# Prologue of a delta-rule and feed-forward kernel: order of its first loads, stores and solves changed, the second solve one step earlier

## The chip, the cores and the metric

The kernel runs on one core of one Trainium2 chip. The metric is the device time of one execution in microseconds (us); the time of a kernel is the median of several executions. A core has TensorE for matrix products (PE in the rows, its weight loads apart as PEld), VectorE (DVE), ScalarE (ACT), GpSimd (POOL) and SyncE (SP). Each engine runs its own instructions in order, and each of SP, ACT and POOL can also issue DMA transfers; an engine that waits, for a semaphore or for room to issue a transfer, holds up all that stands behind on it.

## The reference

```python
# attention, for every batch b and head h (B=4, H=8, S=768, D=48)
k_n = k / (norm(k) + 1e-6)
for t in range(S):
    y[:, :, t] = q[:, :, t] @ state
    v_old = state^T k_n[:, :, t]
    state = state + beta[t] * outer(k_n[:, :, t], v[:, :, t] - v_old)
x = y as (B*S, H*D) = (3072, 384)
# first feed-forward
h = maximum(x @ w_in, 0); x = (h * h) @ w_out          # 384 -> 2048 -> 384
# second feed-forward
h = maximum(maximum(x @ w1, x @ w2), x @ w3)           # 384 -> 768
out = h @ w_out2                                       # 768 -> 384
```

All of it is float32.

## The kernel before

**Tiling.** The 768 positions are cut into 12 chunks of 64, and the recurrence within a chunk becomes triangular algebra: products K K^T and Q K^T of the chunk (`kk_matmul`, L160), a solve of the strict triangle in blocks of 32 (`solve`, L243/L245, 30 pairs of small VectorE operations, scaled at L246), and a few small products with the running state `Sb`. The chunks are solved two at a time (`HALVED`): pair 0 is chunks 0 and 1, pair 1 is chunks 2 and 3, and so on. A chunk is 256 rows of the feed-forward, 64 positions of 4 batches. The heads of a chunk are worked in two halves, p=0 and p=1.

**From K K^T to a solve.** A `kc` load (L149) brings one half of a chunk's keys and queries; `kk_matmul` forms the products; ACT copies K K^T out of PSUM (L175) and VectorE masks Q K^T (L176); K K^T is stored in device memory (`kk`, L164) and so is Q K^T (`p`, L181). `start32` reads `kk` back in the layout of the solve, `buf<-kk` (L262, the "M loads", four for a pair), and `prep` takes the diagonal (`ss`, L224), forms norms (L195 to L208), selects the strict triangle on GpSimd (L213) and scales (L214). After the solve, `finish32` stores the result as `xt` (L278), and each chunk's attention loads it as `xb` (L294).

**Attention of a chunk.** `load_x` and `load_att` load `k` (L291), `xb` (L294), `kq` (L306), `v` (L308), `p` (L310) and `ktp` (L312). Then come the products with the 32-blocks (`pZ` L344, transpose L340, copy L346; `pW` L354, copy L356), `st0` (scaled v L361; for chunks from 1 on `pA`, `pY` from the state L372, and r = v - pA L375), `mm_u` (pU L382, u L383), `st2` (pY L395, pD L400, state update L404/L406, yy L410) and `st3` (transpose L416, and the split of the result into `xh`, `xl`, L419/L420). In `attention` the two halves are worked one after the other, p=0 to its yy before p=1 starts at its `mm_u`.

**First feed-forward.** `moe_a(c)` works the 256 rows of chunk c: for eight pieces fp of 256 hidden columns, `s1` forms the products with `win` (L446), ACT takes relu, square and the high part (`gg`, `p`, `gh`, L451 to L453), VectorE the low part (`gl`, L454), and `s2` multiplies with `wout` (L465). A float32 matrix product is made of three products of high and low parts, so each weight is first split: `convert` (L81 to L100) takes five VectorE operations (L93, L96, L97, L98, L100) and two on ACT (L90, L99) for a piece of 128 columns. The result is stored as `x` (L477), twice per step; twelve steps, one for each chunk, follow each other. The second feed-forward (L619 to L677) starts behind them.

**What sets the order.** In the prologue: K K^T of pair 0, the first `NE` = 5 conversions of `win`, solve of pair 0, attention of chunk 0, the other `win` conversions. Then `steps(moe_a(c), ...)` interleaves step c with generators at given rates: attention of chunk c+1, `wout` conversions in step 0, K K^T of a pair (`KK`), the solve of a pair (`SOLVE`), and from step 9 on the conversions of `w3` weights (`w3load`). A scheduler with a timeline then orders the instructions of each engine by what it thinks is ready; `behind(a, b)` adds an order between two instructions without data. The transfers issued by SP and by ACT share eight semaphores in turn, so an issue also waits for the transfer eight issues before it to have landed; those of POOL have eight of their own.

Pair 0 is done in the prologue. In the kernel before, pair 1 has its K K^T in step 0 and its solve in step 1 (rate 8). Chunk 2's attention, which needs that solve, stands in step 1 too, begun late and at rate 1.3, and its end is in step 2. The scheduler may take conversions of `w3` earlier than their step, where it finds room:

Of the kernel before, what the change touches and what calls it, by code (L numbers as in the profile page):

```python
# [17 lines left out]
NC = S // C  # L18
# [17 lines left out]
def delta_moe(ctx, tc, kc, ab, kt, vt, beta, beta32, beta16, kq, w_in, w_out, w1, w2, w3, w_out2, out):  # L36
# [32 lines left out]
    NR, NRP = 3, 9  # L69
# [11 lines left out]
    def convert(src, hi, lo, shape, lo_eng, dma):  # L81
# [18 lines left out]
        lo_eng.tensor_tensor(out=lo, in0=l.bitcast(F32), in1=hi.bitcast(F32), op=ALU.subtract)  # L100
# [38 lines left out]
    kcs, nk, p_stored, kk_ends = {}, [0, 0], [], [None, None]  # L139
# [5 lines left out]
    def kkp_load(c, p):  # L145
        k = kcts[nk[0] % len(kcts)]
        nk[0] += 1
        kcs[c, p] = k
        nc.sync.dma_start(k, two(kc, c, p).rearrange("p b q t s -> p (b q) t s"))  # L149
# [13 lines left out]
    def kk_store(c, p, kk, dma):  # L163
        return [dma.dma_start(kk_d[c][:, t, U2 * p:U2 * p + U2], kk[64 * t:64 * t + 64]).ins for t in range(2)]  # L164

    def kkps(cs, ps_, dma=nc.sync):
# [4 lines left out]
        for n, (c, p) in enumerate(todo):  # L171
# [4 lines left out]
            kk_ends[1] = vec.tensor_mul(out=ks[:, 1], in0=pq, in1=mask[:, 1].unsqueeze(1).broadcast_to([128, U2, C])).ins  # L176
            yield
            stores = kk_store(c, p, ks[:, 0], dma)
            for t in range(2):
                o = 64 * t  # L180
                stores.append(nc.sync.dma_start(p_d[c][o:o + 64, U2 * p:U2 * p + U2], ks[64 - o:128 - o, 1]).ins)  # L181
            p_stored[:] = stores[2:]
# [34 lines left out]
    selected = [None]  # L217
# [34 lines left out]
    def start32(g, dma=nc.sync):  # L252
# [21 lines left out]
    def finish32(g, M, dma=nc.sync):  # L274
# [44 lines left out]
    ops, normed = [], []  # L319

    def attention(c):
# [36 lines left out]
        def st0(p):  # L358
# [3 lines left out]
            if c < 2:  # L362
                behind(i.ins, ops[-1])
# [23 lines left out]
        def st2(p):  # L387
            pt_, kt_, u_, pY = (tiles[c, p][i] for i in (3, 4, 7, 8))
            if not c:
                pY = ps_y.tile([128, U2, D], F32, name="pY", tag="y")  # L390
# [16 lines left out]
            yy[p] = att.tile([128, Q, 2, D], F32, name="yy", tag="yy", bufs=1)  # L407
# [18 lines left out]
        for fs in ((st0, 0),), ((zz, k21),), ((ww, 0),), ((mm_u, 0),), ((st2, 0),), ((st0, 1), (st3, 0)), ((mm_u, 1),), ((st2, 1),), ((st3, 1),):  # L426
            for f, p in fs:
                f(p)
                if f is mm_u and p and c + 1 < NC:
# [4 lines left out]
    def moe_a(c, gp):  # L434
# [4 lines left out]
        def s1(fp):  # L439
# [14 lines left out]
            vec.tensor_sub(out=gl, in0=p1, in1=gh.bitcast(F32))  # L454
# [73 lines left out]
    if True:  # L528
# [48 lines left out]
        raw_after[:] = raw_done  # L577
        drain(solve32(0, pool))
        x_after.append(selected[0])
        drain(attention(0))  # L580
        x_after.clear()
# [147 lines left out]
```

## Time and profile before

| | us |
|---|---|
| median of 3 executions | 1062.96 |
| lowest, highest | 1060.36, 1063.26 |
| the profiled execution | 1065.6 |
| span of its profile | 1063.9 |
| PE busy in the span | 933.4 (88%) |
| VectorE busy | 477.6 (45%) |
| ACT busy | 395.1 (37%) |

The span is the time from the first to the last instruction that the profiler saw, 1.7 us less than the execution's own time. The steps of the first feed-forward are marked by their first `x` store. These stores begin at 168.1, 213.6, 291.9, 348.8, 397.8, 455.3, 503.3, 560.2, 620.8, 669.5, 716.9 and 758.7 us, so a step is the time between two of them.

### The profile page before, as it was taken

The numbers are of one execution on the slowest core, as the hardware profiler recorded it, in microseconds if no ns is written. First come the engines' busy times: TensorE is split into PE (matmuls) and PEld (weight loads), VectorE is DVE, ScalarE is ACT, GpSimd is POOL, SyncE is SP. The second block draws the span as 40 slices with busy tenths as digits, with TensorE's granted clock in tenths as the row PEclk, the third lists the DMA queues.
The fourth block names the chain that finished last, engine by engine and source line by source line (L and its number), as shares of the span: only waits on it lengthen the run. The fifth ranks groups of instructions, "written<-read, shape, count | busy, mean of one in ns | idle before, by whom it ended". The sixth has DMA issues, their size and how long they took to land.

```text
span 1063.9 us, 26753 instructions
## 1 busy us (share of the span) xinstructions
PE 933.4 (88%) x11706; PEld 856.9 (81%) x11706; DVE 477.6 (45%) x1057; ACT 395.1 (37%) x780; POOL 125.6 (12%) x200
## 2 busy tenths in 40 slices
PE   4004999959998999899988989998999999999998
PEld 4004898948997999799988979998888888888887
DVE  2799937547223841384257641227352323232221
ACT  2126653423443444344454444455431212121111
POOL 1323010130202020202020202000110000000000
PEclk8555898978999899999998989998999999999999
DMA  9954562552245134514452341104220100000001
GB/s 265 291 122 119 174 177 75 139 139 49 73 128 158 49 95 118 159 53 105 116 165 85 82 144 59 34 9 127 89 75 15 45 16 30 15 16 23 8 23 38
DMA packets 89333, 98.44 MB, mean 93 GB/s; under 512 B 49120, under 2 KB 66784, under 8 KB 89216
## 3 DMA queue, kind: packets, MB, share of 16 engines
q1 hardware_dynamic: 74624, 59.36, 20.3%
q0 software_dynamic: 10496, 31.60, 10.1%
q10 hardware_dynamic: 4096, 5.77, 1.6%
q8 instruction: 92, 1.51, 0.6%
q14 instruction: 25, 0.20, 0.1%
HBM read 71.53 MB, written 25.17 MB: 91 GB/s over the span
## 4 chain that ended last, share of the span: by engine, by line
PE 73%; DVE 10%; DMA 10%; issue 3%; ACT 3%; SPq 1%; POOL 1%; DVEq 0%; ACTq 0%; POOLq 0%
PE p L637 21%; PE p L446 17%; PE px L465 17%; PE po L654 7%; DMA buf<-kk 2%; PE pU L382 2%; DMA kk<-big 2%; DVE buf L243 2%; DVE buf L245 2%; DMA raw<-in_moe_w_dram 2%; PE pk L160 1%; PE pW L354 1%; PE pY L395 1%; PE pZ L344 1%; PE pA L372 1%
## 5 line engine op out<-in xcount | busy, mean ns | idle before, releaser
L465 PE MATMUL px<-gh,wout 128*128 128x256 f32 x1152 | 227.3, 296 | 22.3 <-ACT gh L453 22.3
L465 PEld LDWEIGHTS px<-gh,wout 128*128 128x128 f32 x1152 | 187.0, 200 | 26.2 <-ACT gh L453 23.6
L637 PE MATMUL p<-x_h,w 128*128 128x512 f32 x648 | 203.4, 395 | 0.0
L465 PE MATMUL px<-gl,wout 128*128 128x256 f32 x576 | 170.3, 296 | 5.9 <-DVE gl L454 5.8
L446 PE MATMUL p<-xh,win_h 128*128 128x256 f32 x576 | 169.9, 296 | 0.2
L446 PE MATMUL p<-xl,win_h 128*128 128x256 f32 x576 | 167.3, 294 | 0.0
L446 PE MATMUL p<-xh,win_l 128*128 128x256 f32 x576 | 166.3, 289 | 0.0
L454 DVE TENSOR_TENSOR gl<-p,gh 128x512 fp32r<-128x512 f32 x96 | 65.9, 687 | 175.9 <-ACT gh L453 175.4
L637 PEld LDWEIGHTS p<-x_h,w 128*128 128x128 f32 x648 | 121.6, 188 | 27.1
L637 PE MATMUL p<-x_l,w 128*128 128x512 f32 x324 | 128.1, 395 | 0.0
L451 ACT ACTIVATE gg<-p 128x512 f32<-128x512 f32 x96 | 57.1, 596 | 190.8 <-PE p L446 188.4
L465 PEld LDWEIGHTS px<-gl,wout 128*128 128x128 f32 x576 | 115.3, 200 | 8.4 <-DVE gl L454 7.9
L446 PEld LDWEIGHTS p<-xh,win_h 128*128 128x128 f32 x576 | 114.8, 199 | 1.9 <-ACT xh L419 0.7
L446 PEld LDWEIGHTS p<-xh,win_l 128*128 128x128 f32 x576 | 114.6, 199 | 0.0
L446 PEld LDWEIGHTS p<-xl,win_h 128*128 128x128 f32 x576 | 113.2, 198 | 1.6
L643 DVE TENSOR_TENSOR mx<-p,mx 128x512 f32<-128x512 f32 x36 | 24.9, 691 | 137.1 <-PE p L637 137.1
L637 PEld LDWEIGHTS p<-x_l,w 128*128 128x128 f32 x324 | 61.0, 188 | 14.6
L645 ACT CAST hh<-mx 128x512 fp32r<-128x512 f32 x36 | 22.3, 620 | 130.8 <-DVE mx L644 130.8
L245 DVE TENSOR_TENSOR buf<-buf 128x30 f32<-128x30 f32 (+9 forms) x180 | 59.5, 330 | 5.2
L243 DVE TENSOR_TENSOR buf<-buf 128x30 f32<-128x30 f32 (+9 forms) x180 | 59.2, 329 | 5.4
L452 ACT ACTIVATE p<-gg 128x512 f32<-128x512 f32 x96 | 57.6, 601 | 2.7
L453 ACT CAST gh<-p 128x512 fp32r<-128x512 f32 x96 | 56.1, 585 | 2.7
(132 smaller groups left out, 1362.0 us busy)
## 6 DMA issues: line engine op xcount, KB each, us to landing
kq<-in_kc_dram POOLq DMA_DIRECT2D x22, 448.0 KB, 4.1
raw<-in_moe_w_dram SPq DMA_DIRECT2D x18, 384.0 KB, 4.4
p<-p POOLq DMA_DIRECT2D x24, 256.0 KB, 3.3
raw<-in_moe_w_out_dram SPq DMA_DIRECT2D x13, 384.0 KB, 3.7
buf<-in_kc_dram SPq DMA_DIRECT2D x11, 448.0 KB, 3.8
big<-in_kc_dram SPq DMA_DIRECT2D x11, 448.0 KB, 4.3
v<-in_vt_dram POOLq DMA_DIRECT2D x24, 192.0 KB, 3.9
ktp<-in_kt_dram POOLq DMA_DIRECT2D x24, 192.0 KB, 3.4
```

The lines of the kernel that those rows point to most:

```text
L243: eng.tensor_tensor(out=tv, in0=M[:, 0:j, j].unsqueeze(2).broadcast_to([u, j, m]), in1=M[:, j, j + 1:n].unsqueeze(1).broadcast_to([u, j, m ...
L245: yield eng.tensor_tensor(out=M[:, 0:j, j + 1:n], in0=M[:, 0:j, j + 1:n], in1=tv, op=ALU.add)
L446: pe.matmul(p1[:, j], w[:, k, f], x[c][:, k], start=n == 0 and j == 0, stop=n == 8, skip_group_check=True)
L451: act.activation(out=gg, in_=p1, func=AF.Relu)
L452: act.activation(out=p1, in_=gg, func=AF.Square)
L453: act.copy(gh, p1)
L454: vec.tensor_sub(out=gl, in0=p1, in1=gh.bitcast(F32))
L465: pe.matmul(acc[m], w, x[:, j], start=f == 0 and i == 0 and m != 1, stop=f == NF - 1 and i == 2, skip_group_check=True)
L637: pe.matmul(p, w[i][:, k, fs], x[:, k], start=n == 0, stop=n == 8)
L643: vec.tensor_max(out=t, in0=ps[1], in1=t)
L645: act.copy(hh[:, f], t2)
L654: pe.matmul(po[:, 0:DM], x[:, f, js], w[:, f], start=i == 0, stop=i == 17)
```

## The change

In words, in the order of the program:

- Prologue: `NE` is 4 and not 5. The `kk` stores are all on SP (they were on ACT). The `p` stores of pair 0 move from SP to POOL, behind the triangle's selection. Of the four M loads of solve 0, those of chunk 0 stay on POOL, those of chunk 1 go to SP; the `xt` stores of chunk 0 go to ACT, those of chunk 1 stay on POOL. The first operation of `prep` stands behind the last early conversion, and the later `win` loads behind the last M load.
- The K K^T of pair 1 moves from step 0 into the prologue: its `kc` loads stand behind the last `win` load, its mask operations behind the end of solve 0, and it uses four buffers instead of two.
- The attention of chunk 0 works p=0 and p=1 side by side; the second `pY` and `yy` get places of their own.
- Solve 1 moves from step 1 (rate 8) into step 0 (rate 5, begun after 45 turns, its operations behind the eighth `wout` conversion). The K K^T of the later pairs stay in their steps (`KK` loses its entry for step 0), and chunk 2's attention, in step 1, gets the rate of all others.
- The VectorE part of the `w3` conversions stands behind the last `gl` of step 8; this is lifted for step 11.

```diff
-    def kkps(cs, ps_, dma=nc.sync):
+    def kk_store(c, p, kk):
+        for t in range(2):
+            nc.sync.dma_start(kk_d[c][:, t, U2 * p:U2 * p + U2], kk[64 * t:64 * t + 64])
+
+    def kkps(cs, ps_, late_p=None):
...
+            for i in mul_after:
+                behind(kk_ends[1], i)
...
-        vec.tensor_copy(ss, diagonal(M, n))
+        i = vec.tensor_copy(ss, diagonal(M, n))
+        for j in prep_after:
+            behind(i.ins, j)
...
-                dma.dma_start(M[o:o + 32], units(kk_d[c][..., 32 * s:32 * s + 32], 32 * s, 32))
+                loaded[0] = dmas[i].dma_start(M[o:o + 32], units(kk_d[c][..., 32 * s:32 * s + 32], 32 * s, 32)).ins
...
-                dma.dma_start(units(xt_d[c][..., h], 32 * s, 32), M[o:o + 32])
+                dmas[i].dma_start(units(xt_d[c][..., h], 32 * s, 32), M[o:o + 32])
...
+            order = ((st0, 0), (st0, 1)), ((zz, k21),), ((ww, 0),), ((mm_u, 0), (mm_u, 1)), ((st2, 0), (st2, 1)), ((st3, 0), (st3, 1))
...
-        drain(kkps(HALVED[0], (p1, at), act))
-        NE = 5
+        drain(kkps(HALVED[0], (p1, at), ps_stores))
+        NE = 4
...
+        first_solve = solve32(0, (pool, nc.sync), (act, pool))
...
+        mul_after.append(solved[0])
+        kc_after.append(raws[-1])
+        drain(kkps(HALVED[1], (p1, at)))
...
-        KK, SOLVE = {0: 1, 1: 2, 3: 3, 5: 4, 7: 5}, {1: 1, 2: 2, 4: 3, 6: 4, 8: 5}
+        KK, SOLVE = {1: 2, 3: 3, 5: 4, 7: 5}, {0: 1, 2: 2, 4: 3, 6: 4, 8: 5}
...
-                extra.append((1.3, later(11, attention(c + 1))) if c == 1 else (9 / 15.0, attention(c + 1)))
+                extra.append((9 / 15.0, attention(c + 1)))
...
-                extra.append((8.0 if c == 1 else 5.0, solve32(SOLVE[c])))
+                extra.append((5.0, later(45, solve32(SOLVE[c])) if c == 0 else solve32(SOLVE[c])))
...
             if c == 9:
+                after[:] = last_gl
                 load_w3s = w3load((0, 1))
```

What stands where, at three places. The numbers in the names of tiles tell instances apart: `xt_117` and `kk_93` are chunk 0's, `xt_118` and `kk_94` chunk 1's, `kk_95` and `kk_96` those of chunks 2 and 3; `ksr`, `buf` and `big` are buffers. A line number of the changed kernel is some 4 to 20 higher than that of the same code before.

First place: the stores of solve 0's result for chunk 0 (`xt_117`). On POOL, in the kernel before:

```order
L312 DMA ktp_148<-in_kt_dram 128x384
L306 DMA kq<-in_kc_dram 112x1024 x2
L278 DMA xt_117<-buf 32x32x32 x2
L278 DMA xt_118<-buf 32x32x32 x2
L308 DMA v<-in_vt_dram 128x384 x2
L294 DMA xb<-xt_117 32x16x32 x4
```

On ACT, in the changed kernel, from the norms of solve 0 to the same stores:

```order
L205 ACTIVATE s_401<-ss 128x32
L283 COPY normT<-pt 32x32 x4
L91 ACTIVATE cvt<-big 128x384 x2
L180 COPY buf<-pk 128x512
L180 COPY big<-pk 128x512
L180 COPY ksr_194<-pk 128x512
L291 DMA xt_117<-buf 32x32x32 x2
L180 COPY ksr_195<-pk 128x512
```

The two stores of `xt_117` stood on POOL behind the loads of chunk 0's attention; they stand on ACT now, behind three of the four copies of pair 1's K K^T.

Second place: VectorE in the middle of step 0, where `gl` is written for the feed-forward. Before:

```order
L100 TENSOR_TENSOR wout_1214<-raw,wout_1214 128x384
L97 SCALAR_TENSOR_TENSOR raw<-raw,cvt 128x384
L100 TENSOR_TENSOR wout_1214<-big,wout_1214 128x384
L98 SCALAR_TENSOR_TENSOR raw<-raw 128x384
L454 TENSOR_TENSOR gl<-p_1119,gh 128x512
L93 TENSOR_SCALAR cvt<-cvt 128x384
L96 TENSOR_SCALAR cvt<-cvt 128x384
```

The changed kernel, between its third and fourth `gl` of that step:

```order
L474 TENSOR_TENSOR gl<-p_1246,gh 128x512
L258 TENSOR_TENSOR buf<-buf 128x6x25
L99 SCALAR_TENSOR_TENSOR raw<-raw 128x384
L98 SCALAR_TENSOR_TENSOR raw<-raw,cvt 128x384
L94 TENSOR_SCALAR cvt<-cvt 128x384
L256 TENSOR_TENSOR buf<-buf 128x168
L99 SCALAR_TENSOR_TENSOR raw<-raw 128x384
L97 TENSOR_SCALAR cvt<-cvt 128x384
L258 TENSOR_TENSOR buf<-buf 128x7x24
L101 TENSOR_TENSOR wout_1336<-raw,wout_1336 128x384
L98 SCALAR_TENSOR_TENSOR big<-big,cvt 128x384
```

Solve 1's rows (L256/L258, `buf<-buf`) have come in between the conversions and the `gl`; there are 60 of them, the first ahead of the first `gl`, the last right behind the seventh of eight.

Third place: VectorE where the second half of chunk 2's `r` is written, which PE's pU (L382) waits for. Before, at the turn from step 1 to step 2:

```order
L340 STREAM_TRANSPOSE xT<-xb 128x512
L454 TENSOR_TENSOR gl<-p_2558,gh 128x512
L176 TENSOR_TENSOR big<-pq,mask 128x512
L224 COPY ss<-buf 128x32
L404 TENSOR_TENSOR Sb<-pD,Sb 128x384
L195 TENSOR_SCALAR s_2781<-s_2781 128x32
L196 RECIPROCAL r<-s_2781 128x32
L197 TENSOR_TENSOR r<-r,ss 128x32
L198 TENSOR_TENSOR r<-r,s_2781 128x32
L199 TENSOR_SCALAR nm<-r 128x32
L205 RECIPROCAL r<-nm 128x32
L375 TENSOR_TENSOR r<-v,pA 128x384
```

The changed kernel, in step 1, up to the same `ss`:

```order
L474 TENSOR_TENSOR gl<-p_2310,gh 128x512
L417 TENSOR_TENSOR Sb<-pD,Sb 128x384
L181 TENSOR_TENSOR buf<-pq,mask 128x512
L474 TENSOR_TENSOR gl<-p_2429,gh 128x512
L388 TENSOR_TENSOR r<-v,pA 128x384
L436 TENSOR_TENSOR xl<-pT,xh 128x3x128
L374 TENSOR_TENSOR v<-v,normT 128x384
L474 TENSOR_TENSOR gl<-p_2521,gh 128x512
L181 TENSOR_TENSOR big<-pq,mask 128x512
L353 STREAM_TRANSPOSE xT<-xb 128x512
L474 TENSOR_TENSOR gl<-p_2627,gh 128x512
L235 COPY ss<-buf 128x32
```

Before, this `r` stood behind `ss` and six more operations of solve 2's preparation, and `ss` waits for solve 2's M loads; in the changed kernel the same `r` (its line is 388) stands seven rows ahead of that `ss` (L235), among the `gl` of step 1.

## Rows read from the trace of the kernel before

**Rows 1.** Busy time by engine, PE clock, DMA share and GB/s, in stretches of us.

```profile
core 0: us, PE busy (x) PEld busy (x) DVE busy (x) ACT busy (x) POOL busy (x), PEclk, DMA share, GB/s
24.00:60.00 36.00, 0.37 (x1) 0.10 (x1) 28.84 (x78) 5.93 (x15) 9.56 (x15) 0.50 0.99 268
213.60:266.00 52.40, 37.97 (x688) 35.27 (x682) 31.96 (x87) 16.41 (x37) 10.90 (x17) 0.77 0.37 95
26.60:78.50 51.90, 0.39 (x2) 0.15 (x3) 44.23 (x118) 9.32 (x22) 15.49 (x23) 0.50 0.82 212
78.50:112.00 33.50, 18.36 (x382) 15.98 (x383) 32.47 (x83) 21.76 (x47) 8.28 (x10) 0.50 0.43 130
112.00:168.10 56.10, 52.55 (x998) 50.20 (x998) 32.30 (x74) 31.72 (x67) 7.29 (x11) 0.96 0.55 156
168.10:291.90 123.80, 108.82 (x1718) 103.14 (x1720) 68.31 (x174) 45.11 (x91) 20.61 (x33) 0.88 0.37 97
291.90:397.80 105.90, 100.43 (x1752) 95.56 (x1747) 47.41 (x111) 45.84 (x94) 18.07 (x29) 0.97 0.38 107
...
503.30:560.20 56.90, 52.35 (x1005) 49.63 (x999) 21.35 (x44) 27.39 (x55) 9.65 (x15) 0.97 0.49 139
560.20:620.80 60.60, 54.64 (x781) 50.94 (x774) 42.15 (x113) 28.65 (x61) 8.43 (x14) 0.92 0.35 99
620.80:669.50 48.70, 46.09 (x729) 43.88 (x731) 13.68 (x26) 21.94 (x44) 8.43 (x14) 0.96 0.29 88
```

**Rows 2.** What PE waited for, 0 to 112 us: total, times, longest.

```profile
PE pZ L344 <- DMA xb<-xt: 38.1, 1, 38.1
PE pt L235 <- DVE nm L199: 20.8, 1, 20.8
```

**Rows 3.** Chain of waits, 0 to 112 us: start, duration, what.

```profile
11.06 7.71 DMA buf<-in_kc_dram
18.79 3.97 DMA kk<-big
...
28.17 8.83 DMA buf<-kk
37.60 1.09 DVE s L195
...
65.50 1.02 DVE r L361 x2
```

**Rows 4.** DMA issues from 24 to 60 us: KB each, median us to landing.

```profile
buf<-kk POOLq DMA_DIRECT2D x4, 128.0 KB, 8.7
```

**Rows 5.** Store of xt (L278) and load of xb, to landing: min, median, max.

```profile
DMA to landing us min/median/max: 2.4/4.1/5.5
...
DMA to landing us min/median/max: 5.0/6.4/7.0
```

**Rows 6.** VectorE's timeline before step 0: start, duration, what.

```profile
110.13 0.55 DVE L420 TENSOR_TENSOR xl<-pT,xh 128x384 fp32r<-128x384 f32 x1
```

**Rows 7.** What PE waited for in steps 1 and 2.

```profile
PE pU L382 <- DVE r L375: 7.9, 1, 7.9
PE pA L372 <- DVE Sb L404: 3.5, 1, 3.5
```

**Rows 8.** What VectorE waited for, 213.6 to 266 us.

```profile
DVE ss L224 <- DMA buf<-kk: 7.7, 1, 7.7
```

**Rows 9.** VectorE in step 8 by line: busy, mean ns, idle before.

```profile
L245 DVE TENSOR_TENSOR buf<-buf 128x30 f32<-128x30 f32 (+14 forms) x30 | 9.8, 328 | 0.6
...
L100 DVE TENSOR_TENSOR w<-raw,w 128x384 fp32r<-128x384 f32 x7 | 3.7, 547 | 4.5 <-ACT w L99 4.5
```

**Rows 10.** What ACT waited for, 503 to 670 us.

```profile
ACT cvt L90 <- DMA raw<-in_moe_w_dram: 9.6, 6, 3.1
...
ACT w L99 <- DMA xt<-buf: 5.2, 1, 5.2
ACT w L99 <- DMA p<-big: 4.8, 1, 4.8
```

More of the change, by code (lines that the diff above doesn't have):

```diff
@@ L148, in kkp_load @@
         kcs[c, p] = k
-        nc.sync.dma_start(k, two(kc, c, p).rearrange("p b q t s -> p (b q) t s"))
+        i = nc.sync.dma_start(k, two(kc, c, p).rearrange("p b q t s -> p (b q) t s"))
+        for j in kc_after:
+            behind(i.ins, j)
     def kk_matmul(c, p, ps_):
@@ L176, in kkps, with p_store @@
             kk_ends[1] = vec.tensor_mul(out=ks[:, 1], in0=pq, in1=mask[:, 1].unsqueeze(1).broadcast_to([128, U2, C])).ins
+            for i in mul_after:
+                behind(kk_ends[1], i)
             yield
[L178 to L182, printed above, removed]
+            kk_store(c, p, ks[:, 0])
+            def p_store(dma, c=c, p=p, ks=ks):
+                return [dma.dma_start(p_d[c][64 * t:64 * t + 64, U2 * p:U2 * p + U2], ks[64 - 64 * t:128 - 64 * t, 1]).ins for t in range(2)]
+            if late_p is None:
+                p_store(nc.sync)
+            else:
+                late_p.append(p_store)
             if n + ahead < len(todo):
@@ L318, in delta_moe @@
     xh, xl = {}, {}
-    ops, normed = [], []
+    ops, normed, solved, solve_after = [], [], [], []
     def attention(c):
@@ L362, in st0 @@
             if c < 2:
-                behind(i.ins, ops[-1])
+                behind(i.ins, solved[0])
             if not c:
@@ L406, in st2 @@
                     vec.tensor_copy(sv, pD)
-            yy[p] = att.tile([128, Q, 2, D], F32, name="yy", tag="yy", bufs=1)
+            if p and not c:
+                yy[p] = pkp.tile([128, Q, 2, D], F32, name="yy1", tag="yy1")
+            else:
+                yy[p] = att.tile([128, Q, 2, D], F32, name="yy", tag="yy", bufs=1)
             for i in range(2):
@@ L425, in attention @@
         load_att(c, 1)
-        for fs in ((st0, 0),), ((zz, k21),), ((ww, 0),), ((mm_u, 0),), ((st2, 0),), ((st0, 1), (st3, 0)), ((mm_u, 1),), ((st2, 1),), ((st3, 1),):
+        if c:
+            order = ((st0, 0),), ((zz, k21),), ((ww, 0),), ((mm_u, 0),), ((st2, 0),), ((st0, 1), (st3, 0)), ((mm_u, 1),), ((st2, 1),), ((st3, 1),)
+        else:
+            order = ((st0, 0), (st0, 1)), ((zz, k21),), ((ww, 0),), ((mm_u, 0), (mm_u, 1)), ((st2, 0), (st2, 1)), ((st3, 0), (st3, 1))
+        for fs in order:
             for f, p in fs:
                 f(p)
-                if f is mm_u and p and c + 1 < NC:
+                if f is (mm_u if c else st2) and p and c + 1 < NC:
                     load_att(c + 1, 0)
@@ L546, in delta_moe, with solve32 @@
             behind(pool.memset(t_, 0.0).ins, i_mask.ins)
-        def solve32(g, *dma):
-            M, a, norm = start32(g, *dma)
+        def solve32(g, load=(nc.sync, nc.sync), store=(nc.sync, nc.sync)):
+            M, a, norm = start32(g, load)
             normed.append(norm())
@@ L552, in solve32 @@
             for i in solve(vec, M, 32, 64 * len(HALVED[g]), a, tmp32):
+                for j in solve_after:
+                    behind(i.ins, j)
                 ops.append(i.ins)
                 yield
-            finish32(g, M, *dma)
+            finish32(g, M, store)
         def later(n, g):
@@ L576, in delta_moe @@
             load_win(f, vec, nc.sync)
[L577 to L581, printed above, removed]
+        prep_after.append(parted[-1])
+        first_solve = solve32(0, (pool, nc.sync), (act, pool))
+        next(first_solve)
+        prep_after.clear()
+        raw_after[:] = loaded
+        stores = [i for f in ps_stores for i in f(pool)]
+        for i in stores:
+            behind(i, selected[0])
+        drain(first_solve)
+        solved.append(ops[-1])
+        x_after.append(stores[-1])
         after[:], abs_after[:] = ops[-1:], normed[0:1]
```

31 lines of the change are left out of this document (20 added, 11 removed).

## The prediction

> **What bounds the kernel now.** I read the view by stretches first, then the waits of PE, and last, for each large wait, the chain of waits there. In nearly every step PE is the engine with the least slack: 100.43 of 105.90 us in steps 3 and 4, at a clock of 0.97 [rows 1]. Three places are different. Up to 78.5 us PE does almost nothing; its longest wait is 38.1 us for the first `xb<-xt` [rows 2], so the prologue lasts as long as the chain K K^T, `kk`, M loads, solve, `xt`, `xb`. From there to 112 us VectorE is busy 32.47 of 33.50 us with conversions [rows 1]: that stretch is as long as VectorE's list. And steps 1 and 2 take 123.80 us against 105.90 us for steps 3 and 4 [rows 1], which do the same kind of work (a K K^T in the first, a solve in the second).
>
> The chain in the prologue starts late for a reason off the chain. ACT's second `kk` store could not be issued until an early `kc` load, a prefetch of step 0's K K^T, had landed (7.71 us, from 11.06 to 18.77); behind that store ACT's later copies queue up, then come 3.97 us for `kk<-big` and 8.83 us for the M load `buf<-kk`, and `ss` is only done ahead of 37.60 us [rows 3]. A pair of the same loads later takes less: the DMA engines are 0.99 busy from 24 to 60 us at 268 GB/s [rows 1], the M loads' median is 8.7 us there [rows 4].
>
> **Prologue: the early part.** The change takes away the `kc` prefetches and the fifth early `win` load, and takes the `kk` stores off ACT. PE's K K^T then follows its four `kc` loads without a break. The chain in front of 18.79 us [rows 3] shrinks by the wait for that prefetch, about 7 us; the M load falls from 8.83 us towards the 3.97 us of `kk<-big` [rows 3], about 4.5 us; the fifth conversion (about five VectorE operations at 32.47 / 83 = 0.39 us, so 2 us [rows 1]) and one early store behind another give the rest. I get `ss` at about 23.3 us in place of 37.1: minus 14 us. The solve's own length stays (37.6 to 65.5, with its end marked by the `r` that is ordered behind it [rows 3]), so it ends near 51.7.
>
> Here the change sends the M loads from two engines. The Trainium skill ("DMA: Bandwidth & Descriptors", section "Issuing engines are not separate DMA queues") says that transfers started by different engines run on the same 16 DMA engines, interleave, and gain only the time of the issue. The row agrees: the four M loads had POOL's own queue to themselves and still took 8.7 us beside SP's `win` loads [rows 4]. By that rule the gain of 14 us comes from what is no longer ahead, and not from the second queue; were the queues separate, the prologue's whole 14 us would reach step 0, which is the first rival below.
>
> **Prologue: what takes the gain back.** Moving the solve forward doesn't move the bytes. Behind the last M load there now stand twelve `win` loads of 384 KB (tiles of 128 x 768, four bytes), four `kc` loads of 448 KB for pair 1 that were in step 0, four `p` stores of 128 KB on POOL, attention's `kq`, `v`, `p`, `ktp` and `k` for chunk 0 (2.7 MB), and on SP four `wout` loads and one more `kc`: together 11.9 MB. At 268 GB/s [rows 1] that is 44 us, from about 23.5 to 68. The `xt` stores of chunk 0 now stand on ACT behind three copies of pair 1's K K^T. Those copies need the third of the new `kc` loads, by when about 8.9 MB must have passed: 23.5 + 33 = 56.5 us; with the matmuls and copies, about 59. The issue itself then waits for a transfer eight issues earlier on the semaphores that SP and ACT share, which is a `kc` or `kk` transfer of the same crowd. I take 62.5 us, between 59 and 68. Before, the same store could go at 65.6 and pZ followed 12.9 us later, at 78.5 (the end of pZ's 38.1 us wait [rows 1, 2]): 4.1 us for the store and 6.4 us for the load [rows 5], and the issues. So pZ goes at about 75, 3.5 us earlier.
>
> From there VectorE's list decides. Its rows from the transpose to the second `xl` number about 80 before and 84 in the changed order, at 0.39 us each 31 to 33 us: the second `xl`, before at 110.13 [rows 6], comes at about 107. Working p=0 and p=1 side by side takes away PE's waits between the halves, but those end behind the same list, so I cost it at nothing: VectorE's conversions cover it, and if these were gone it would be worth a few us. Two more edits wait on the same engine: `ss` of solve 1 now stands in that list and waits for M loads that SP can issue only late, behind two `wout` loads (price 0 to 5 us), and the mask operations of pair 1 stand in front of the conversions and wait for the `kc` loads. **Term A: -3.5 us, between +2 and -14.**
>
> **Step 0.** It lasts 56 us from 112 with PE busy 52.55 and VectorE 32.30 [rows 1]. VectorE loses four masks and gains solve 1: 60 operations of 0.33 us (9.8 us for 30 [rows 9]), 20 us, with preparation and scaling about 23, of which the first ten operations fall into the prologue. That makes about 51 us: as long as PE, which loses the K K^T, about 4 us. In the changed order VectorE has 104 rows from the first `gl` to the eighth, at 0.39 us 40 us; with 12 us ahead of them and 3 to 5 us behind, step 0 takes 55 to 58 us. **Term B: -0.5 us, between -4 and +8**, the upper end if the `gl` wait makes PE wait too.
>
> **Steps 1 and 2.** What made them 17.9 us longer than steps 3 and 4 is the late solve 1. Chunk 2's attention could not begin before its end, ran into step 2 with few other matmuls beside it, and its `r` stood behind solve 2's `ss`, which waited 7.7 us for its M loads [rows 8]; PE waited 7.9 us for that `r` and 3.5 us for the next state [rows 7]. The clock was 0.77 over that stretch of 52.40 us, in which PE was busy for 37.97 [rows 1]. With solve 1 done in step 0, chunk 2's `r` stands ahead of that `ss`, and the steps 1 and 2 have the form that steps 3 and 4 have now. **Term C: 105.9 - 123.8 = -17.9 us, between -14 and -19.** At the lower gain, chunk 2's `xb` comes a few us late: its `xt` stores go only after solve 1's last row, right behind the seventh `gl`, 4.1 + 6.4 us [rows 5] ahead of `xb`, and PE wants it about three us later than that.
>
> **Steps 7 to 10.** Most of the `w3` conversions ran ahead of their step: seven in step 8 [rows 9], more in step 7. There ACT waited for their loads (9.6 us) and, through shared semaphores, for `xt<-buf` and `p<-big` (5.2 and 4.8 us) [rows 10]; step 7 and 8 take 117.5 us against the 105.9 of steps 3 and 4 [rows 1]. Their VectorE part now stands behind step 8's last `gl`, so these 11.6 us go, and steps 9 and 10 get the twelve conversions. Step 9 takes 48.70 us with VectorE busy 13.68 and ACT 21.94 [rows 1], so there is room, but ACT waits in order there too for raw loads ahead of its `gg`, up to 3.1 us at a time [rows 10]; two of those per step give back 6. **Term D: -5 us, between 0 and -10.**
>
> **The sum.** -3.5 - 0.5 - 17.9 - 5 = -26.9 us. On the profiled execution, 1065.6 us, that is 1038.7. That execution is 2.6 us above the median of the runs, so the forecast is 1036.
>
> **The rivals.** (a) The prologue's gain comes through in full. For it: nothing but the order of loads holds `xt`, and 128 KB could slip through among larger transfers. Against it: the M loads did not (8.7 us [rows 4]), and the three copies stand ahead. Then A is -14: 1036 - 10.5 = 1025.5. (b) Step 0 becomes VectorE's. For it: 51 us of VectorE against 48 of PE, and `ss` of solve 1 can wait for its loads. If A is 0 and B +8: 1036 + 3.5 + 8.5 = 1048. (c) Slower than before. One mechanism: the solve's operations in step 0 space the `gl` so far apart that PE falls to half its clock (0.50 from 78.5 to 112, where it was busy 18.36 of 33.50 us [rows 1]) and stays there. At half of the 2.4 GHz step 0's 48 us of matmuls approach 90, so the step grows by over 33 us: 1036 + 33 = 1069. It decides once step 0 is longer than about 83 us, so half clock for most of it. Against it: PE would have 85% of its time busy even in (b), and at 0.77 with 37.97 of 52.40 busy the clock still came back [rows 1]. (d) The change does not do what it says in steps 1 and 2: `xb` of chunk 2 late by so much that the wait only moves (C -5, D 0): 1036 + 13 + 5 = 1054.
>
> **How the numbers follow.** Forecast 0.50, with its own range 1030 to 1043; (a) 0.18; (b) 0.17; (d) 0.08; within 0.3% of the time before, which is about 3 us and what a measurement of this kernel can tell from no change, 0.03; (c) 0.04. Faster by more than that: 0.50 + 0.18 + 0.17 + 0.08 = 0.93. The range of 8 in 10 goes from 1022, a little below (a), to 1052, above (b).
>
> **What would show it.** Right: `ss` near 23 us, solve 0's end near 52, ACT's `xt` store held until about 60, pZ near 75, a first `x` store near 164, steps 1 and 2 at 106 with no wait of pU for `r`, no `w` conversions in step 8. Wrong: pZ near 65 (a), a step 0 of over 62 us (b) or 83 us (c), a long pZ wait in step 1 (d), or new ACT waits on raw `w` loads in step 9 of over 10 us.

## The result and the profile after

The changed kernel takes 1042.83 us (median of 4 executions, 1042.10 to 1043.73) beside 1061.66 us of the kernel before (4 executions). The ratio is 0.9825, with a 95% interval from 0.9805 to 0.9846: 18.8 us less, where 26.9 were forecast. The time lies within the stated range of 1022 to 1052. The profiled execution took 1042.8 us with a span of 1041.1 us, 22.8 us less than the span before; that the two profiles differ by 4 us more than the medians is because the profiled execution of before, at 1065.6 us, was slower than the median of its kernel.

In the changed kernel the first `x` store of each step is at L497, and the first two come at 173.8 and 229.4 us. Busy time by stretch shows two parts of the prologue, its last part, step 0 and the eight `gl` within it (129.10 to 168.80), steps 1 and 2, and then steps 7, 8 and 9 one by one; the columns are those of [rows 1].

```profile
core 0: us, PE busy (x) PEld busy (x) DVE busy (x) ACT busy (x) POOL busy (x), PEclk, DMA share, GB/s
...
24.00:68.00 44.00, 10.17 (x257) 9.35 (x257) 32.80 (x90) 4.71 (x12) 14.04 (x23) 0.50 1.04 302
...
54.00:78.50 24.50, 9.80 (x256) 9.28 (x257) 14.84 (x33) 6.13 (x12) 5.47 (x8) 0.50 0.98 271
78.50:113.50 35.00, 17.41 (x391) 15.64 (x392) 30.67 (x83) 19.86 (x43) 8.03 (x11) 0.55 0.40 93
113.50:173.80 60.30, 53.20 (x749) 50.36 (x748) 49.68 (x131) 32.42 (x69) 5.78 (x10) 0.87 0.39 123
129.10:168.80 39.70, 39.23 (x555) 37.71 (x555) 36.05 (x98) 23.88 (x52) 4.67 (x8) 0.91 0.25 74
173.80:277.80 104.00, 98.75 (x1703) 94.19 (x1705) 47.71 (x111) 45.38 (x92) 20.80 (x33) 0.97 0.43 113
...
487.40:542.90 55.50, 52.24 (x995) 49.53 (x991) 18.11 (x39) 23.90 (x49) 9.67 (x15) 0.97 0.45 121
542.90:591.00 48.10, 47.75 (x796) 45.51 (x796) 33.51 (x85) 23.77 (x50) 8.43 (x14) 1.00 0.29 76
591.00:646.30 55.30, 48.77 (x711) 45.92 (x713) 33.12 (x70) 30.17 (x63) 8.46 (x14) 0.94 0.47 142
```

Set beside the stretches of [rows 1], this is where the time went, by the two profiles:

| stretch | before | after | difference | forecast |
|---|---|---|---|---|
| start to the second `xl` of chunk 0 | 110.1 | 113.5 | +3.3 | -3.5 (A) |
| second `xl` to the first `x` store | 58.0 | 60.4 | +2.4 | -0.5 (B) |
| steps 1 and 2 | 123.8 | 103.9 | -19.9 | -17.9 (C) |
| steps 3 to 6 | 211.4 | 209.8 | -1.6 | 0 |
| steps 7 and 8 | 117.5 | 103.6 | -13.9 | |
| steps 9 and 10 | 96.1 | 103.0 | +6.9 | -5 with the row above (D) |
| the rest | 347 | 347 | 0 | 0 |

What PE and VectorE waited for up to step 0 tells why the first two rows have the wrong sign. First PE, from 0 to 112 us (total, times, longest), to be read against [rows 2]:

```profile
PE pk L163 <- DMA buf<-in_kc_dram: 25.0, 1, 25.0
PE pZ L357 <- DMA xb<-xt: 12.2, 2, 12.1
PE pt L248 <- DVE nm L210: 12.0, 1, 12.0
PE pU L395 <- ACT xb L369: 6.3, 1, 6.3
```

and VectorE, from 55 to 114 us:

```profile
DVE ksr L181 <- PE pq L163: 5.7, 1, 5.7
DVE ss L235 <- DMA buf<-kk: 4.3, 1, 4.3
```

The wait for solve 0's norms (`nm`) has fallen from 20.8 to 12.0 us: the early part works. But the 38.1 us before pZ are only cut in two, by the K K^T of pair 1, which PE itself awaits for 25.0 us; and pZ still starts at 78.5 us. VectorE now waits for those matmuls (5.7 us) and for solve 1's loads (4.3 us). ACT's timeline (start, duration, what, idle before) shows the `xt` stores of chunk 0, which solve 0's end at 55.0 would have allowed:

```profile
56.93 0.59 ACT L180 COPY buf<-pk 128x512 f32<-128x512 f32 x1 [25.22 <-issue]
58.79 0.59 ACT L180 COPY big<-pk 128x512 f32<-128x512 f32 x1 [1.27 <-PE pq L163]
60.60 0.59 ACT L180 COPY ksr<-pk 128x512 f32<-128x512 f32 x1 [1.22 <-PE pk L163]
68.74 1.12 ACTq L291 DMA_DIRECT2D xt<-buf  x2
```

They go at 68.74 us: behind three copies of pair 1, and then 7.5 us later still. The trace has what they waited for. The first of them waits on the semaphore of a `kc` load that SP issued at 58.47 us, eight issues earlier. SP had issued pair 1's four `kc` loads by 39.2 us, so this one belongs to the next pair. It landed 10.2 us later, at 68.64, 0.1 us ahead of the store:

```profile
L150 SPq DMA_DIRECT2D buf<-in_kc_dram x1: 333/333/333, 58.5 to 58.5; - x1
...
DMA to landing us min/median/max: 10.2/10.2/10.2
```

This is the kind of wait that the change took away from ACT's `kk` store [rows 3], back at another store of ACT.

In step 0 PE waits once for long, for ACT's `gh`, where its longest wait in that step was 2.5 us before. ACT stands at a conversion until its `wout` load lands, with the first `gg` and `gh` of the step behind it:

```profile
PE px L485 <- ACT gh L473: 6.6, 1, 6.6
```

```profile
120.53 0.56 ACT L91 ACTIVATE cvt<-raw 128x384 f32<-128x384 f32 x1 [5.47 <-DMA raw<-in_moe_w_out_dram]
...
127.66 0.61 ACT L473 CAST gh<-p 128x512 fp32r<-128x512 f32 x1
```

PE's wait ends at 128.3 us. From the first `gl` (129.1) to the end of the eighth (168.8) PE is busy for 39.23 of 39.70 us and VectorE for 36.05, so PE has the least slack there.

### The profile page after: what moved, and what is told of

It reads as the page before. It is cut to its first block, busy times and chain, and to the rows that moved or that the text cites. A ratio compares the mean times of both kernels' runs of the same rounds, so it can differ in the third digit from the quotient of the medians.

```text
span 1041.1 us, 26747 instructions
## 1 busy us (share of the span) xinstructions
PE 926.8 (89%) x11706; PEld 851.2 (82%) x11706; DVE 479.1 (46%) x1057; ACT 394.3 (38%) x780; POOL 125.5 (12%) x204
## 3 DMA queue, kind: packets, MB, share of 16 engines
q1 hardware_dynamic: 76704, 59.62, 20.8%
## 4 chain that ended last, share of the span: by engine, by line
PE 67%; DMA 13%; issue 7%; DVE 6%; ACT 3%; SPq 2%; POOL 2%; DVEq 0%; POOLq 0%; ACTq 0%
PE p L680 22%; PE p L466 14%; PE px L485 14%; PE po L697 7%; DMA raw<-in_moe_w_dram 3%; DMA buf<-kk 2%; PE pU L395 2%; DMA rawp<-in_moe_w_in_dram 2%; DMA raw<-in_moe_w_out_dram 2%; DMA kk<-big 2%; DMA v<-in_vt_dram 1%; SPq L88 1%; PE pY L408 1%; PE pk L163 1%; PE pZ L357 1%
## 5 line engine op out<-in xcount | busy, mean ns | idle before, releaser
L258 DVE TENSOR_TENSOR buf<-buf 128x30 f32<-128x30 f32 (+9 forms) x180 | 59.4, 330 | 5.2
L256 DVE TENSOR_TENSOR buf<-buf 128x30 f32<-128x30 f32 (+9 forms) x180 | 59.3, 329 | 5.4
```

The source lines that it names most:

```text
L256: eng.tensor_tensor(out=tv, in0=M[:, 0:j, j].unsqueeze(2).broadcast_to([u, j, m]), in1=M[:, j, j + 1:n].unsqueeze(1).broadcast_to([u, j, m ...
L258: yield eng.tensor_tensor(out=M[:, 0:j, j + 1:n], in0=M[:, 0:j, j + 1:n], in1=tv, op=ALU.add)
```

## The experiments

Each kernel was run beside the kernel before, which took 1061.3 to 1061.8 us each time. The scatter was larger than in the first runs, some 3 us about a median and up to 6 for the kernel before, so differences of 3 us between two experiments are not told apart; where a stretch of a profile says more than the median, the text says so.

**The xt stores of chunk 0 on POOL.**

```diff
-        first_solve = solve32(0, (pool, nc.sync), (act, pool))
+        first_solve = solve32(0, (pool, nc.sync), (pool, pool))
```

> One part undone: the xt stores of chunk 0 go back from ACT to POOL; all else as in the changed kernel. Theory (the store behind three K K^T copies on ACT, issued at 68.7 us, is what keeps pZ at 78.5): the store goes at about 55, right behind solve 0's end, pZ comes near 70 to 72, and the second xl a few us earlier (solve 1's ss, which waits for its loads until 88 us, still stands in VectorE's list): 1038 to 1042 us. Rival (VectorE's list of conversions and masks alone sets the second xl): pZ may come earlier, the second xl stays at 113, 1043 us.

Measured 1039.6 us. The stores go at 56.6 us and pZ comes at 73.2, but the second `xl` only at 112.1, 1.3 us earlier; VectorE's waits hardly change:

```profile
DVE ksr L181 <- PE pq L163: 6.0, 1, 6.0
DVE ss L235 <- DMA buf<-kk: 4.8, 1, 4.8
```

The store on ACT is what held pZ, by 5 us; it isn't what held the second `xl`. So the theory is right on pZ, and the rival on the `xl`. The first `x` store came 6.5 us earlier all the same, from a step 0 of 55.2 us, in which PE waits 1.5 us for ACT's `gh` and not 6.6.

**Solve 1's preparation behind the second xl.**

```diff
-            vec.tensor_sub(out=xl[c][:, :, 128 * p:128 * (p + 1)], in0=pv, in1=hi.bitcast(F32))
+            i = vec.tensor_sub(out=xl[c][:, :, 128 * p:128 * (p + 1)], in0=pv, in1=hi.bitcast(F32))
+            if p and not c:
+                prep_after.append(i.ins)
...
+                prep_after.clear()
```

> One order added: the first operation of solve 1's preparation (ss) stands behind the second xl of chunk 0. Theory (ss of solve 1 idles VectorE for 4.3 us in the prologue, and POOL's selection behind it holds back the xb loads of chunk 1): pU no longer waits 6.3 us, the second xl comes near 106 to 108 in place of 113.5, and step 0, which gets the preparation of about 4 us, keeps most of that: 1037 to 1040 us. Rival (step 0 is as long as VectorE's list, so whatever leaves the prologue is paid there): step 0 grows by the same 5 to 7 us, 1042 to 1045 us.

Measured 1035.7 us, 7 us less than the changed kernel. The second `xl` comes at 107.1 and `pU` waits 0.7 us. Step 0 and step 1 by stretch:

```profile
107.10:157.90 50.80, 50.38 (x729) 47.68 (x728) 48.50 (x132) 31.97 (x70) 8.62 (x11) 0.93 0.44 142
157.90:222.20 64.30, 56.83 (x987) 53.81 (x979) 21.62 (x49) 23.97 (x48) 12.25 (x19) 0.88 0.52 131
```

Step 0 didn't grow, as the rival had it; it shrank to 50.8 us, and PE is busy for all of it: its wait for `gh` is down to 0.2 us, with VectorE's work in the step nearly as before (48.50 us, 49.68 in the changed kernel). But solve 1 ends at 162 us, after that step, so step 1 grew from 55.6 to 64.3 us and gave back more than half of the 15.9 us that the first `x` store had gained.

**Both together.** The edits of the two kernels above.

> Both at once: xt stores of chunk 0 on POOL, and solve 1's preparation behind the second xl. Theory: the two add up, second xl near 100 to 103, 1031 to 1036 us. Rival (VectorE's list sets it): not better than the better one of the two alone, within 2 us.

Measured 1036.0 us: not better than the second edit alone. pZ at 74.3, second `xl` at 105.9, first `x` store at 160.7. The rival holds.

**The w3 conversions free again.**

```diff
-                after[:] = last_gl
                 load_w3s = w3load((0, 1))
```

> One part undone: the w3 conversions are not held behind step 8's last gl. Theory (this edit is worth 14 us in steps 7 and 8 and costs 7 in steps 9 and 10): steps 7 and 8 go back to about 117 us, steps 9 and 10 to 96, 1048 to 1051 us. Rival (steps 7 and 8 are shorter because of the changed order before them, and the edit only moves the conversions): 1041 to 1044 us.

Measured 1050.5 us, as the theory had it, but not for its reason. Steps 7 and 8 took 111.6 us (+8.0 on the changed kernel) and steps 9 and 10 92.8 (-10.2), which together would be a small gain. The loss is in step 1, 65.4 us in place of 55.6: without the edit the scheduler's order came out differently in step 0 too, with more conversions between solve 1's rows; the solve ended 5 us later (at 176 us), and PE waited for chunk 2's `xb`. What PE waited for from 173.4 to 238.8 us, and the stretch:

```profile
PE pZ L357 <- DMA xb<-xt: 5.2, 1, 5.2
```

```profile
173.40:238.80 65.40, 54.67 (x1041) 51.85 (x1033) 19.28 (x40) 25.13 (x54) 12.26 (x19) 0.93 0.52 128
```

This is the danger that rival (d) named: PE waits 5.2 us, the mean clock over the step is 0.93 instead of 0.99, and the step is 9.8 us longer. That the other order of step 0 made the solve late is argued; only the times are shown.

**The w3 edit alone, on the kernel before.**

```diff
+            last_gl[0] = vec.tensor_sub(out=gl, in0=p1, in1=gh.bitcast(F32)).ins
...
             if c == 9:
+                after[:] = last_gl
                 load_w3s = w3load((0, 1))
...
+                after.clear()
                 extra.append((0.5, w3load((2,))))
```

> One part alone: the kernel before, with the VectorE part of the w3 conversions held behind step 8's last gl. Theory (term D as forecast, -5, measured as -7 between the two profiles): steps 7 and 8 shrink by 11 to 14 us, steps 9 and 10 grow by 5 to 8, 1053 to 1057 us. Rival (the edit only moves the conversions, or costs a little, as steps 7 to 11 of the kernel with this edit undone took 2.8 us less than with it): 1060 to 1065 us.

Measured 1060.5 us beside 1061.5, ratio 0.9993 with an interval from 0.9967 to 1.0018: no difference that can be told. The stretches of steps 7 to 10 show the conversions moving, 12.4 us out of the first pair and 8.2 into the second:

```profile
503.00:559.90 56.90, 52.18 (x1003) 49.46 (x999) 19.26 (x43) 23.82 (x49) 9.65 (x15) 0.97 0.45 118
559.90:608.10 48.20, 47.65 (x777) 45.21 (x768) 32.70 (x82) 23.51 (x51) 8.40 (x14) 1.00 0.30 76
608.10:665.00 56.90, 51.07 (x724) 48.23 (x728) 32.78 (x70) 30.19 (x63) 8.54 (x14) 0.91 0.48 138
665.00:712.40 47.40, 47.34 (x667) 45.38 (x659) 10.18 (x16) 23.64 (x47) 0.00 (x0) 1.00 0.03 10
```

The rival holds: the edit moves the conversions. In this profile the four steps are 4.2 us shorter than in that of the kernel before, but that one was an execution 4 us slower than its median.

**Pair 1 back in steps 0 to 2.** The prologue's early part stays.

```diff
-        drain(kkps(HALVED[1], (p1, at)))
...
-        KK, SOLVE = {1: 2, 3: 3, 5: 4, 7: 5}, {0: 1, 2: 2, 4: 3, 6: 4, 8: 5}
+        KK, SOLVE = {0: 1, 1: 2, 3: 3, 5: 4, 7: 5}, {1: 1, 2: 2, 4: 3, 6: 4, 8: 5}
...
-                extra.append((9 / 15.0, attention(c + 1)))
+                extra.append((1.3, later(11, attention(c + 1))) if c == 1 else (9 / 15.0, attention(c + 1)))
...
-                extra.append((5.0, later(45, solve32(SOLVE[c])) if c == 0 else solve32(SOLVE[c])))
...
+                extra.append((8.0 if c == 1 else 5.0, solve32(SOLVE[c])))
```

> One part undone: K K^T of pair 1 back in step 0, solve 1 back in step 1 at rate 8, chunk 2's attention late and at rate 1.3; the prologue's early part, the side by side halves and the w3 order stay. Theory (moving pair 1 forward is worth 18 to 20 us in steps 1 and 2 and costs the prologue and step 0 about 14): the xt store on ACT goes at about 55, pZ near 70, the first x store near 160, steps 1 and 2 take about 122 us, 1046 to 1052 us. Rival (the late solve is not what made steps 1 and 2 long): steps 1 and 2 stay at 104 to 108, 1028 to 1034 us. Second rival (the early part gives nothing by itself, VectorE's list sets the first x store near 168): 1055 to 1060 us.

Measured 1054.6 us, ratio 0.9931 (0.9906 to 0.9955); expected 1046 to 1052, so a little over the theory's range and just short of its second rival's (from 1055). The prologue and steps 1 and 2 behave as the theory says. ACT's `xt` stores, and the stretches from pZ to the second `xl`, step 0, and steps 1 and 2:

```profile
55.84 0.96 ACTq L291 DMA_DIRECT2D xt<-buf  x2
```

```profile
65.20:95.90 30.70, 19.38 (x398) 17.07 (x398) 30.63 (x79) 20.83 (x46) 7.05 (x11) 0.50 0.24 69
95.90:158.80 62.90, 54.72 (x935) 52.12 (x937) 36.87 (x86) 32.42 (x67) 6.76 (x11) 0.89 0.65 186
158.80:285.10 126.30, 108.88 (x1769) 103.01 (x1767) 68.16 (x171) 47.13 (x98) 20.66 (x33) 0.89 0.37 95
```

The store goes at 55.8 us, pZ comes at 65.2, the second `xl` at 95.4: the early part by itself is worth 14.8 us at that point. That this is close to the 14 us that the prediction gave it is in part luck: the 14 stood for `ss`, which starts at 27.6 us, only 9.5 earlier than before; solve 0 ends 9.8 us earlier, and pZ comes 13.3 earlier, since it follows solve 0's end by 9.4 us where that took 12.9. The first `x` store at 158.8, and not near 168, speaks against the second rival. Over a third of the 14.8 us is lost in a step 0 of 63 us: its `wout` loads fall into the same time (DMA share 0.65), ACT waits 5.7 us for one of them and PE 6.8 us for `gh`. Pair 1, moved forward, costs 18 us at the second `xl` and 15 at the first `x` store, and saves 22 in steps 1 and 2.

**All M loads of solve 0 on POOL.**

```diff
-        first_solve = solve32(0, (pool, nc.sync), (act, pool))
+        first_solve = solve32(0, (pool, pool), (act, pool))
```

> One part undone: all four M loads of solve 0 on POOL. Theory (all transfers share the same engines; the second queue saves only the time of the issue): ss of solve 0 at most 2 us later or earlier, pZ and the first x store within 1 us, 1041 to 1045 us. Rival (the second queue is what makes the loads fast): ss 4 us or more later, and the store of xt with it.

Measured 1045.6 us. The rival on `ss` holds: solve 0 ends at 63.4 us, 8.4 later. What SP issues around 20 us shows why, first in the changed kernel, then here:

```profile
22.53 0.96 SPq L275 DMA_DIRECT2D buf<-kk  x2
23.53 0.57 SPq L88 DMA_DIRECT2D big<-in_moe_w_in_dram  x1
```

```profile
20.38 1.19 SPq L88 DMA_DIRECT2D big<-in_moe_w_in_dram  x2
21.61 0.61 SPq L88 DMA_DIRECT2D buf<-in_moe_w_in_dram  x1
22.26 1.07 SPq L88 DMA_DIRECT2D rawp<-in_moe_w_in_dram  x1
```

The M loads on SP wait there for `kk`, and SP, in order, holds back its `win` loads with them. With the M loads on POOL, six `win` loads are issued ahead of the last two, and their median time to landing rises from 3.8 us (POOL) and 3.1 us (SP) to 6.9 us:

```profile
buf<-kk POOLq DMA_DIRECT2D x2, 128.0 KB, 3.8
buf<-kk SPq DMA_DIRECT2D x2, 128.0 KB, 3.1
```

```profile
buf<-kk POOLq DMA_DIRECT2D x4, 128.0 KB, 6.9
```

And yet pZ comes at 78.2 and the second `xl` at 113.1, as in the changed kernel: 8.4 us at the end of solve 0 are worth nothing at that point while pair 1's loads set what follows. The first `x` store comes 6.5 us earlier than in the changed kernel, but solve 1 ends at 170.7 as there (170.8), PE waits 2.8 us for chunk 2's `xb`, and the second `x` store comes at 229.1 beside 229.4.

**The halves of chunk 0 one after the other.**

```diff
-        if c:
+        if True:
             order = ((st0, 0),), ((zz, k21),), ((ww, 0),), ((mm_u, 0),), ((st2, 0),), ((st0, 1), (st3, 0)), ((mm_u, 1),), ((st2, 1),), ((st3, 1),)
```

> One part undone: the halves of chunk 0's attention one after the other again. Theory (VectorE's list covers it, cost put at nothing in the prediction): second xl within 3 us of 113.5, 1040 to 1046 us. Rival (side by side is worth the waits between the halves, 9 us before): second xl near 120, 1048 to 1052 us.

Measured 1046.7 us in four runs from 1041.3 to 1049.4, which leaves its worth open between 0 and a few us. The second `xl` comes at 113.1 us as before, so in the prologue the edit costs and brings nothing, as the prediction had it.

**Eight wout operations on POOL.**

```diff
-                load_wout(f, vec, nc.sync)
+                load_wout(f, pool if f >= 8 else vec, nc.sync)
```

> The changed kernel with one cost moved: the last operation of the last eight wout conversions goes from VectorE to POOL, eight times 0.47 us. Theory (from solve 0's end to the eighth gl of step 0 VectorE's list sets the time): the eighth gl and the first x store come 3 to 4 us earlier, solve 1 ends earlier too, 1038 to 1041 us. Rival (PE sets step 0): no change, 1042 to 1044 us; second rival: POOL's slower operation makes the px matmuls of step 0 wait, 1045 us or more.

Measured 1053.2 us, 10 us slower than the changed kernel, in the direction of the second rival. The eighth `gl` ends at 169.6 us, against 168.8. VectorE has eight operations fewer in step 0 and is busy as long (49.87 us, 49.68 in the changed kernel). By line (busy, mean ns), in the changed kernel and here:

```profile
L97 DVE TENSOR_SCALAR cvt<-cvt 128x384 int32<-128x384 int32 x9 | 3.2, 355 | 0.0
```

```profile
L97 DVE TENSOR_SCALAR cvt<-cvt 128x384 int32<-128x384 int32 x9 | 5.0, 556 | 0.0
```

The timeline has it one by one: while POOL works from 131.25 us on, VectorE's next two operations take 1.1 us each in place of about 0.3:

```profile
131.25 2.12 POOL L101 TENSOR_TENSOR wout<-big,wout 128x384 fp32r<-128x384 f32 x2 [1.95 <-ACT wout L100]
```

```profile
131.37 1.13 DVE L97 TENSOR_SCALAR cvt<-cvt 128x384 int32<-128x384 int32 x1
132.42 1.08 DVE L256 TENSOR_TENSOR buf<-buf 128x108 f32<-128x108 f32 x1
```

So what was taken off VectorE comes back as longer operations, and nothing is gained. Step 0 isn't where the time is lost: the first `x` store comes at 172.5 us, 1.3 earlier than in the changed kernel. The second comes 5.7 us later, behind a step 1 of 62.6 us, in which PE waits 4.3 us for a `gl`. Why that `gl` is late, and where the rest of the 10 us goes, is open.

**The same move with solve 1's preparation behind the second xl.** The edits of that kernel and of the one above.

> The same move on top of solve 1's preparation behind the second xl (1035.7 us without it). Theory: step 0 and what of solve 1 reaches into step 1 shorten by up to 4 us, 1032 to 1035 us. Rival (step 0 is now at PE's own length, 50.8 us): 1035 to 1037 us.

Measured 1040.7 us (1038.8 to 1044.9) where 1035.7 (1033.7 to 1040.6) were measured without the move: neither theory nor rival. The move seems to cost here too, but the two ranges overlap.

**The masks of pair 1 later**, with the xt stores on POOL and solve 1's preparation behind the second `xl`.

```diff
-        mul_after.append(solved[0])
+        mul_after.append(parted[7])
```

> On top of both earlier edits (xt stores of chunk 0 on POOL, solve 1's preparation behind the second xl; 1036.0 us): the masks of pair 1's K K^T stand behind the eighth win conversion instead of the end of solve 0. Theory (VectorE stands idle for 6 us there because it waits in order for the matmuls of loads that have not landed): most of the 6 us goes, second xl near 101 in place of 105.9, 1031 to 1034 us. Rival (the conversions wait for their own loads, or pZ for xb, by as much): 1035 to 1037 us.

Measured 1032.8 us (1029.3 to 1036.3), ratio 0.9725 (0.9683 to 0.9766): the fastest kernel here, by 29 us on the kernel before and 10 on the changed one, though not surely apart from the 1035.7 and 1036.0 above. Its profiled execution, at 1036.3, is the slowest of its four and no faster than those of these two kernels, so the trace doesn't show a gain. Its reason isn't the one given: the second `xl` is at 105.2 us, where 105.9 was measured without the edit. The wait went to the next resource, ACT, which stands in order behind the K K^T copies. What VectorE waited for from 54 to 106 us:

```profile
DVE cvt L94 <- ACT cvt L91: 8.9, 1, 8.9
```

**The masks later and the eight operations on POOL.**

> The masks behind the eighth win conversion and the eight wout operations on POOL, with both earlier edits. Theory: the savings on VectorE add up, 1028 to 1032 us. Rival (one of them ends behind PE or behind a load): not better than the better of the two by over 1 us.

Measured 1039.0 us (1037.8 to 1045.2): the operations on POOL cost here as well, and the rival holds.

## Why the prediction was right, and where its terms were off

**Right:** the mechanism in its main lines. The early part is worth 14.8 us at the second `xl` with pair 1 out of the way, pair 1's loads, copies and operations take it back, and the gain comes from steps 1 and 2, which were long because solve 1 was late. With pair 1 put back, those steps take 126.3 us again, with it moved 103.9. The total lies in the range in part because the terms miss in both directions: in the profiles A and B are 9.7 us worse than forecast, C, D and steps 3 to 6 together 5.6 better.

**Term A** was -3.5 with +2 as its end, and is +3.3, outside its own bounds. It was -14 for the early part and 10.5 for what takes it back; measured at the second `xl` these are -14.8 and 18.1, so the price of pair 1 is what was too low. Its steps, one by one: solve 0's end, 51.7 forecast, 55.0 measured (SP's M loads could be issued only at 22.5 us, when `kk` had landed); ACT's `xt` store 62.5 (59 to 68), measured 68.7; pZ 75, measured 78.5. The transfers went on at 302 GB/s from 24 to 68 us, not at 268, which is 13.3 MB where 11.9 were counted, and they did not end there: the DMA engines are 0.98 busy from 54 to 78.5 us. The count had left out pair 1's own `kk` and `p` stores, which SP issues from 60.6 us on. Of the 6.2 us that the store is late, 2 are the copies (the third ended at 61.2, 59 forecast) and 4 the wait for the landing of the `kc` load (7.5, 3.5 forecast). As the experiment with the store on POOL shows, that was only part of it: with pZ at 73.2 the second `xl` still comes at 112.1. The larger miss is solve 1's preparation: `ss` had the price "0 to 5 us", which was then left out of the sum. It measured 4.3 us of idle VectorE, with the preparation's own operations besides; pU waited 6.3 us, and 0.7 with the preparation moved. Taking it out gave 6.4 us at the second `xl`. That pU waited because POOL's `xb` loads stand behind solve 1's selection was the theory of that experiment; its edit moves both at once.

**Term B** was -0.5 (-4 to +8) and is +2.4. Its VectorE load is right (49.68 us busy, 51 forecast), and so is the time from the first `gl` to the eighth (39 us, 40 forecast). But the reason given, that step 0 becomes as long as VectorE's list, doesn't hold: PE is busy for nearly all of those 39 us. What was too low is the part ahead of the first `gl`, 15.6 us where 12 were forecast, and there PE waits 6.6 us for `gh`, behind ACT's wait for a `wout` load; the working has no such wait. With that wait at 0.2 us, and nearly the same work for VectorE, step 0 took 50.8 us. The first `x` store, forecast near 164 us, came at 173.8.

It looks as if VectorE's work explained the prologue and step 0 together: from solve 0's end to the eighth `gl` it grew from 72.87 us in the kernel before to 91.69 in the changed one, and the stretch from 93.9 to 113.8 us. But the experiments say otherwise. First the two kernels, then the one with solve 1's preparation late, then the one with pair 1 put back:

```profile
65.60:159.50 93.90, 64.79 (x1298) 60.59 (x1299) 72.87 (x173) 55.52 (x113) 21.37 (x30) 0.73 0.56 154
```

```profile
55.00:168.80 113.80, 75.34 (x1302) 70.66 (x1303) 91.69 (x240) 56.94 (x120) 19.28 (x29) 0.69 0.51 144
```

```profile
56.40:155.00 98.60, 72.58 (x1277) 67.55 (x1270) 87.02 (x224) 56.08 (x120) 20.63 (x29) 0.74 0.58 166
```

```profile
55.80:154.60 98.80, 69.91 (x1305) 65.22 (x1305) 72.56 (x172) 55.61 (x116) 19.19 (x29) 0.74 0.56 151
```

The last two stretches are equally long, with 87.02 and 72.56 us of work for VectorE. So the 19.9 us are not the length of VectorE's list alone; the waits inside the stretch, for loads and for ACT, count as well.

**Term C** was -17.9 (-14 to -19), and is -19.9 in the profiles; 22.4 us against the kernel with pair 1 put back. PE no longer waits for `r` in these steps; its longest wait there is 3.9 us, for solve 2's norms (`nm`), at the end of step 1. The margin for chunk 2's `xb`, put at about three us, is as narrow as stated: where the solve ended 5 us later, step 1 was 9.8 us longer.

**Term D** was -5 (0 to -10), and is -7.0 between the two profiles. But the edit alone makes no measurable difference, and undone in the changed kernel it makes steps 7 to 10 2.2 us shorter. The part of the working that says ACT's waits "go" from steps 7 and 8 is right, but in step 9, where nearly all of the conversions now stand, ACT waits 12.6 us for raw loads:

```profile
ACT cvt L91 <- DMA raw<-in_moe_w_dram: 12.6, 6, 4.9
```

That is over the 10 us which the prediction had named as a sign of being wrong. And the step of the working that turns ACT's waits into time of the steps fails: with the edit undone ACT waits 11.6 us for raw loads and 5.7 and 2.2 for `p<-big` and `xt<-buf` in steps 7 to 10, and these are no longer for it. So the size of D was right for the profiles by chance. Where the 7 us come from is open; the profiled execution of before took 4 us more than its kernel's median.

**The two queues.** The prediction said that the gain at solve 0 does not come from the second queue. The row behind that (8.7 us for M loads beside `win` loads [rows 4]) is borne out: two M loads on POOL that had `win` loads ahead of them took 8.4 and 9.2 us. But the conclusion was wrong. Two M loads in SP's own order keep SP's `win` loads behind them, and that is worth 8.4 us at solve 0's end. The Trainium skill ("DMA: Bandwidth & Descriptors", section "Issuing engines are not separate DMA queues") says that transfers of all issuing engines share the same DMA engines and that starting them from several saves only the time of the issue. The first agrees with the 8.4 and 9.2 us; the second doesn't hold here, where the order of issue on SP made the difference.

**What is left of the difference.** The forecast for the profiled execution was 1038.7, and the profiled execution of the changed kernel took 1042.8: 4.1 us more, of which A makes +6.8, B +2.9, C -2.0, D -2.0 and the steps 3 to 6 -1.6. The medians lie 6.8 us apart, because the 2.6 us taken off for the slow profiled execution of before had no counterpart in the changed kernel's.

## What to carry to other kernels

Where one engine's list seems to set a stretch, add up that list from the last point at which it is free to the point that somebody waits for, with each wait in order inside it, and then look for a kernel with the same list and another time: here it was the waits, and not the list alone. A step moved forward takes its loads, copies and stores along, and whatever stands behind these on an in-order engine, here the store that pZ waited for, gets later by as much. Transfers that must go first are put in the same engine's order as the ones that must not pass them.

## What the runs showed of the hardware

VectorE's operations were drawn out while POOL worked on tensors of its own: a 128 x 384 operation took 1.13 us where it took 0.35, a 128 x 108 one 1.08 where 0.27 was usual, so moving eight operations of 0.55 us to POOL, where they took 1.0 to 1.8 us, took nothing off VectorE's busy time in step 0 (49.87 us, 49.68 without the move).

A wait of PE goes with more than itself. In five kernels PE waited 2.7 to 5.2 us at a time for chunk 2's `xb` or for a `gl`, 7 to 15 us into step 1; there the mean clock over the step was 0.88 to 0.93 and the step 6 to 10 us longer than in the changed kernel, with 0.99. In three others, with waits of 2.9 to 3.7 us for `gh`, it was 0.92 to 0.95 and 1 to 5 us. The changed kernel has a wait of 3.9 us as well, for `nm`, but it ends at 227.5 us, shortly before step 2 begins, and so the lower clock falls into step 2. Two stretches show the clock. The first is of the kernel with the w3 conversions free again, where PE waits until 187.3 us, the second of the changed kernel:

```profile
185.50:192.30 6.80, 4.45 (x21) 4.34 (x22) 2.48 (x4) 0.00 (x0) 0.00 (x0) 0.50 0.35 83
```

```profile
228.40:235.30 6.90, 6.66 (x55) 6.18 (x48) 6.28 (x21) 0.75 (x2) 1.12 (x2) 0.51 0.51 156
```

In both the granted clock is at the lower of its two levels, 1.2 GHz; in the changed kernel it is 1.00 from 173.8 to 228.4 us.
